# Attention loop: value and output products in halves of the array's rows, query and key products whole in one step

## The chip, the cores and the metric

The kernel runs on one core of a Trainium2 chip. The metric is the device time of one execution in microseconds (us), from start to end, as the median of several runs. A profile of one execution gives the start and length of every instruction on every engine: TensorE (PE for its products and transposes, PEld for its weight loads), VectorE (DVE), ScalarE (ACT), GpSimd (POOL) and SyncE (SP, which issues the transfers).

## The reference

Four layers follow each other, each on a layer-normalised input and added to it: A, B, A, B, with the same weights for both A and for both B. A is a linear attention with a learned feature map. B, which the change touches, is a causal attention over 4 segments of 512 tokens with 32 heads of 16, and a memory that carries what earlier segments held:

```python
for s in range(N):                                   # N = 4 segments of L = 512
    qs, ks, vs = q[:, :, s], k[:, :, s], v[:, :, s]  # x @ wq, x @ wk, x @ wv
    logits = jnp.einsum("bhqd,bhkd->bhqk", qs, ks) * scale + mask
    p = _softmax(logits, axis=-1)
    a_dot = jnp.einsum("bhqk,bhkd->bhqd", p, vs)
    pq = phi(qs)
    num = jnp.einsum("bhld,bhde->bhle", pq, M)
    den = jnp.einsum("bhld,bhd->bhl", pq, z)[..., None] + 1e-6
    o = g * num / den + (1.0 - g) * a_dot
    outs.append(o)
    pk = phi(ks)
    M = M + jnp.einsum("bhld,bhle->bhde", pk, vs)
    z = z + jnp.einsum("bhld->bhd", pk)
...
return o @ wo
```

## The kernel before

**Stages.** Layer A runs in two passes (`pass1`, `pass2`). Layer B is one hand-ordered loop, `LayerB.steps` (L1470), which also takes in the end of the layer A before it and, in the first of the two layers B, the beginning of the next layer A.

**The loop.** Each of the 4 segments has 4 chunks of 8 heads (128 features), and each chunk two halves (a half chunk, m, is 4 heads: 8 of them a segment, 32 a layer). A half chunk has R = 5 steps; step number k = 5m + j. In every step TensorE does first the query-key products of one piece (`attend`, into the two banks lg, from which ScalarE writes the exponentials P), then those of another piece nine steps ahead for the row maxima (`maxima`, into one bank each, mx and my, of which VectorE takes the maxima). These use 64 rows of the array (63 for the maxima) and come in pairs, one product in the upper and one in the lower half of the rows. Then come the effects due at this step, and the products that fill it.

**What fills the steps.** P times values (`weighted`, bank pv, in column strips of 32) stands in steps j = 0 and 2. The rest is set by the tables FIRST (segment 0), GAPS (segments 1 and 2), LAST and FINAL (segment 3 of the first and the second layer B). An entry "m.j" lists what step j of half chunk m does: q, k, v with a chunk or tile number are the query, key and value projections ("+" for those of the next segment), out the output product of the segment before, max the transpose of the row maxima, t the transpose of key features to tokens, m the update of the memory, a its reading, n and ln the next normalisation (whose last four calls transpose the normalised rows into columns, `columns`, L433), x the request of a residual tile. "/2" takes two quarters of a product: each product is 12 full-array matmuls of 512 columns (`mm3`, L482), four quarters of three, since each operand is kept as a high and a low part and three of the four combinations are summed. "~" puts the VectorE part of its end off into the next step.

**Orders.** All matmuls and transposes of TensorE are held in program order (`held`, L190); so are the instructions of VectorE, ScalarE, GpSimd and the SyncE queue (`Ordered`). The order in which a step issues its work is the order on each engine. In steps j = 2 the deferred VectorE parts (`late`) run before pv and the activations of key and query features (`later`) behind it.

**Banks.** The results of projections, output products, transposes, memory reads and updates share one pool of three PSUM banks, g (G = 3, L33). lg has two banks, mx, my and pv one each.

**Ends.** A projection (`proj`, L1043) ends with the load of the next weights, ScalarE's copy to the high part, VectorE's subtraction for the low part (ta), and, where the memory needs the features, two activations on ScalarE (tb) and two GpSimd instructions. A value product ends with a copy on ScalarE (`v_tile`, L531), an output product with an addition on VectorE and a store (`out`, L1420).

Of the kernel before, what the change touches and what calls it, by code (L numbers as in the profile page):

```python
# [7 lines left out]
F32 = mybir.dt.float32  # L8
# [69 lines left out]


FIRST = """  # L80
0.1 max k2/2 | 0.2 v3/2 | 0.3 k2/2~ | 0.4 v3/2
1.0 m0 | 1.1 max q3/2 | 1.3 q3/2~ | 1.4 t1 k3/1
2.1 max k3/3 | 2.2 m1 w | 2.3 ln~ | 2.4 ln~ ln~
3.1 ln~ max | 3.3 q0+/2 | 3.4 t2 q0+/2~ w
4.0 w | 4.1 max k0+/2 load | 4.2 m2 | 4.3 k0+/1 | 4.4 k0+/1
5.0 n | 5.1 max v0+/4 | 5.2 w | 5.3 q1+/2 n | 5.4 t3 q1+/2~
6.1 max v1+/4 | 6.2 m3 n | 6.3 k1+/2 | 6.4 a0+ k1+/2
7.0 n | 7.1 max q2+/4~ | 7.2 n | 7.3 v2+/2 n | 7.4 t0+ v2+/2
# [12 lines left out]
LAST = """  # L101
0.1 max k2/3~ | 0.2 n | 0.3 k2/1~ v3/2 n | 0.4 a1 v3/2 n
1.0 n | 1.1 max q3/3 n | 1.2 n | 1.3 q3/1~ k3/2 n | 1.4 k3/2~ n
2.1 max out/1 | 2.3 out/2 | 2.4 a2 x0 pre
3.1 max ln~ ln~ | 3.3 pre out/1 ln~ out/1 x1 | 3.4 out/1 ln~
4.1 max out/2~ v/2 | 4.3 pre out/3 x2 | 4.4 a3 out/1~ v/2 x3
5.1 max out/3 | 5.2 out/1 v/1 | 5.3 fin v/1 | 5.4 v/2 pre
6.1 max v/2 | 6.3 fin v/2 | 6.4 v/2
7.1 pt p/3 v/2 | 7.2 v/2 | 7.3 fin v/2 p/3 | 7.4 p/3
"""  # L110
FINAL = """
0.1 max k2/4~ | 0.3 v3/3 | 0.4 a1 v3/1~
1.1 max q3/2 | 1.3 q3/2~ | 1.4 k3/1
2.1 max k3/2 | 2.3 k3/1 out/1 pre | 2.4 a2 out/2 x0
3.0 x1 | 3.1 max | 3.3 pre out/2 | 3.4 out/2
4.1 max out/1~ | 4.3 pre out/2 x2 | 4.4 a3 out/2
5.1 x3 out/2 max | 5.3 fin out/2 | 5.4 pre
6.1 max | 6.3 fin
7.1 pt p/2 | 7.3 p/4 fin | 7.4 p/3
"""  # L120
BEFORE = {-25: "q0 load", -23: "v0", -21: "k0", -18: "n", -17: "v1 n", -16: "n", -15: "n n", -14: "q1 n", -13: "n", -12: "k1 n n", -10: "v2 n", -4: "max q2~", -1: "t0"}


@with_exitstack
def interleave_kernel(ctx, tc, x_in, a_wqkv, a_wphi, a_wo, b_wq, b_wk, b_wv, b_wo, b_beta,
# [15 lines left out]
    def nm(s):  # L141
        uid[0] += 1
        return f"{s}_{uid[0]}"
# [20 lines left out]
    def behind(i, j):  # L164

        tc.add_manual_dep(i.ins, j.ins.name,
                          mybir.DependencyInfo(mybir.DependencyClass.NoSync, mybir.DependencyReason.DATA),
                          reason="keeps order")

    class Ordered:  # L170

# [53 lines left out]
    gated = cp.tile([P, NC, 4], F32, name="gated")  # L225
    ones = cp.tile([32, P], F32, name="ones")
    stats = cp.tile([P, NT, 4], F32, name="stats")
    junk = cp.tile([P, 2, 384], mybir.dt.uint8, name="junk")

    def constants():  # L230
# [776 lines left out]
    class LayerB:  # L1007
# [21 lines left out]

        def values(self, s):  # L1030

            self.vv[s] = []
            yield from v_tile(self.hT[s], self.wv, self.vv[s], ("g", G), (0, 3, 1, 2), True)

        def queue_w(self):

            if self.wnext:
# [2 lines left out]
                dma(w, wqk[m][:, c])  # L1040
                self.w4.append(w)

        def proj(self, s, c, m):  # L1043

            d, hT, w = self.st.setdefault((s, c), {}), self.hT[s], self.w4.pop(0)
            pp = PS("g", G)
            yield from mm3(pp, lambda a, kc: w[:, a, kc, :], lambda b, kc: hT[b][:, kc, :])
            self.queue_w()
            hi, lo = d["part", m] = [T2("ta1", TA, F32R) for _ in range(2)]
            act.copy(hi, pp)  # L1050
            wait(lambda: dve.tensor_tensor(out=lo, in0=pp, in1=hi.bitcast(F32), op=SUB))
            if not (s == 0 if m == 0 else s == NSEG - 1):
                e = d["phi", m] = T2("tb2", TB2)
                r = T2("tb3", 2)

                def first():
                    act.activation(e, pp, AF.Exp)

                def second():
                    act.activation(r, pp, AF.Relu)  # L1060
                    pool.tensor_scalar(e, e, 1.0, None, op0=MIN)
                    pool.tensor_tensor(out=e, in0=e, in1=r, op=ADD)
                self.later += [first, (lambda: self.later.append(second)) if s < 2 else second]
            yield

        def at(self, k, f, *a):

# [351 lines left out]

        def out(self, s):  # L1420
            for t in range(4):
                po = PS("g", G)
                yield from self.product(po, s, t, range(NC))
# [5 lines left out]
                wait(end)  # L1429
                yield  # L1430

        def early(self):

# [18 lines left out]
                yield  # L1452

        def opening(self):
            self.w4 = []
            self.wo = []
            self.wnext = [(m, c) for _ in range(NSEG) for c in range(NC) for m in range(2)]
            for _ in range(2):
                self.queue_w()
                yield  # L1460
            self.wv = []
            yield from bring(self.wv, "bwv")
            self.norm0 = self.norm(0)
            next(self.norm0)
            fills = self.start()
            for n in (0, 0, 1, 0, 1, 0, 1, 1, 1, 1, 0, 1, 1, 1, 1, 1, 1, 1, 1):
                yield
                next(self.norm0 if n else fills, None)

        def steps(self, side, after, table_end):  # L1470
# [8 lines left out]
            outs, proj, part = {}, {}, {}  # L1479
            early = self.early()  # L1480

            def do(what, s, k):
                put_off[0] = self.late if what[-1] == "~" else None
# [8 lines left out]
                elif op == "fin":  # L1492
                    if k >= FINAT:
                        self.finish((k - FINAT) // R)
                elif op in ("q", "k", "v", "out", "p"):
                    if op == "p":
                        g = early
                    elif op == "out":
                        if s == 0:
                            return  # L1500
                        g = outs.setdefault(s, self.out(s - 1))
                    elif op == "v":
                        g = after if i is None else val[s]
                    else:
                        g = proj.setdefault((s, i, op), self.proj(s, i, "qk".index(op)))
# [56 lines left out]
            for k in range(BEGIN, R * N + 4):  # L1562
                m = k // R + 3
                if k % R == 0 and 0 <= m < N:
                    self.stack(m)
                if 0 <= k < R * N:
                    next(at)
                if -LEAD <= k < R * N - LEAD:
                    next(ma)
                put_off[0] = None  # L1570
                self.due(k)
                for s, c in memory["a"].get(k, ()):
                    if s > 0:
# [19 lines left out]
                what, s = table.get(k, ((), 0))  # L1593
# [73 lines left out]
```

## Time and profile before

| What | Value |
|---|---|
| median of 3 runs | 1403.85 us (1402.75 to 1408.85) |
| span of the profiled execution | 1401.3 us |
| instructions | 33234 |
| attention loop, first layer, four segments | 293.0 to 717.0 us |
| attention loop, second layer | 979.6 to 1388.7 us |
| granted TensorE clock | 1.00 throughout |

The profiled execution's span runs from its first to its last instruction; the 2.55 us between it and the median are what lies around it, and the spread of the runs. The costliest groups of the page are ScalarE's exponentials (324.5 us of busy time) and, on TensorE, the full-array products into g. Matmuls are pipelined: the busy time of a group counts an instruction from its start to the end of its results, so that the distance between two starts, not the length, says what an instruction costs TensorE.

### The profile page before, as it was taken

Reading aid. Unit: us, or ns where it says so; the run is one execution under the profiler, and the core shown is the slowest. Engines: PE = TensorE matmul, PEld = TensorE weight load, DVE = VectorE, ACT = ScalarE, POOL = GpSimd, SP = SyncE. Lnnn points to the kernel's source line nnn. Section 1 sums busy time; section 2 is a strip of 40 time slices with the busy share of each in tenths; the row PEclk is TensorE's granted clock in tenths of the full one; section 3 lists DMA queues with packets and bytes.
Section 4 is the critical chain, followed back from the end, with each engine's and each line's share of the span. In section 5 each row is a group of like instructions: output and inputs, shape, how many; then the busy total and the mean of one; then the engine's idle time right before and its main releaser. Section 6 shows DMA issues by size and latency. Waiting matters only on the chain.

```text
span 1401.3 us, 33234 instructions
## 1 busy us (share of the span) xinstructions
PE 1369.1 (98%) x12070; PEld 943.2 (67%) x12070; DVE 963.9 (69%) x3030; ACT 810.9 (58%) x1244; POOL 734.1 (52%) x1073
## 2 busy tenths in 40 slices
PE   9999999999999999999999999999999999999998
PEld 7787778766666666655568887886655666666554
DVE  5766888677667657667647768958776666666674
ACT  5555445447686677566544434553566866765654
POOL 1677755324656656554534346642356565754643
PEclk9999999999999999999999999999999999999999
DMA  5369285645756656567631104855465566565552
GB/s 199 118 216 330 99 280 175 187 122 162 201 131 190 169 137 183 158 171 196 197 134 39 62 31 125 275 162 155 137 172 171 148 178 180 143 172 142 155 158 69
DMA packets 135730, 225.27 MB, mean 161 GB/s; under 512 B 21328, under 2 KB 39888, under 8 KB 135568
## 3 DMA queue, kind: packets, MB, share of 16 engines
q1 hardware_dynamic: 134464, 222.91, 54.2%
q8 instruction: 97, 1.59, 0.5%
q14 instruction: 65, 0.53, 0.1%
q10 hardware_dynamic: 1104, 0.24, 0.1%
HBM read 116.39 MB, written 43.25 MB: 114 GB/s over the span
## 4 chain that ended last, share of the span: by engine, by line
PE 78%; DVE 8%; ACT 5%; POOL 4%; issue 2%; DMA 2%; SPq 0%; DVEq 0%; ACTq 0%; POOLq 0%
PE g L202 47%; PE pv L202 9%; PE lg L202 9%; PE mx L202 4%; PE g L206 3%; PE my L202 3%; ACT P L180 2%; PE lg L206 1%; POOL P L180 1%; POOL tb L180 1%; DVE es L180 1%; POOL tmp L180 1%; DVE junk L180 1%; DVE my L180 1%; DVE mx L180 1%
## 5 line engine op out<-in xcount | busy, mean ns | idle before, releaser
L180 ACT ACTIVATE P<-lg 128x1024 f32<-128x1024 f32 x316 | 324.5, 1027 | 167.5 <-PE lg L202 159.6
L180 POOL TENSOR_SCALAR_AFFINE_SELECT P<-P 128x256 f32<-128x256 f32 (+1 forms) x448 | 190.3, 439 | 388.9 <-ACT P L180 388.1
L180 DVE CUSTOM_DVE_ANT_0 junk<-mx,mask 128x128 uint8<-128x128 f32 (+2 forms) x384 | 146.6, 420 | 101.8 <-PE my L202 72.7
L202 PE MATMUL g<-hh,wqk 128*128 128x512 f32 x512 | 186.3, 411 | 0.7 <-ACT mt L180 0.7
L202 PE MATMUL lg<-e,e 64*128 64x512 f32 (+1 forms) x1010 | 166.0, 386 | 6.4 <-ACT P L180 6.0
L180 DVE CUSTOM_DVE_ANT_0 mx<-mx,mask 128x512 f32<-128x512 f32 x128 | 89.2, 697 | 120.1 <-PE my L202 95.4
L202 PE MATMUL g<-w,oh 128*128 128x512 f32 x508 | 169.2, 414 | 0.5 <-ACT hh L180 0.4
L202 PE MATMUL pv<-P,v 128*32 128x512 f32 (+3 forms) x2048 | 165.5, 439 | 0.6 <-ACT ot L180 0.5
L202 PE MATMUL my<-e,e 63*128 63x256 f32 (+3 forms) x519 | 147.2, 343 | 4.2 <-DVE mxs L180 3.0
L202 PEld LDWEIGHTS lg<-e,e 64*128 64x128 f32 x1010 | 79.9, 184 | 102.9 <-issue 44.9
L202 PE MATMUL mx<-e,e 63*128 63x256 f32 (+3 forms) x519 | 145.9, 334 | 1.9 <-DVE mxs L180 1.6
L180 DVE CUSTOM_DVE_ANT_0 junk<-my,mask 128x128 uint8<-128x128 f32 (+2 forms) x384 | 146.8, 420 | 0.0
L202 PE MATMUL g<-w,hh 128*128 128x512 f32 x448 | 143.9, 402 | 0.3 <-ACT hh L180 0.3
L202 PEld LDWEIGHTS pv<-P,v 128*32 128x32 f32 x2048 | 53.5, 109 | 102.9 <-issue 95.3
L202 PEld LDWEIGHTS g<-hh,wqk 128*128 128x128 f32 x512 | 96.2, 188 | 33.7 <-issue 13.4
L202 PEld LDWEIGHTS g<-w,oh 128*128 128x128 f32 x508 | 87.6, 189 | 30.8 <-issue 13.4
L202 PE MATMUL g<-w,ol 128*128 128x512 f32 x254 | 100.8, 397 | 2.3 <-DVE ol L180 2.2
L180 DVE DVE_READ_ACCUMULATOR2_ANT mxs<- 128x1 f32 x1024 | 100.4, 98 | 0.0
L202 PE MATMUL g<-hl,wqk 128*128 128x512 f32 x256 | 100.3, 392 | 0.0
L202 PEld LDWEIGHTS mx<-e,e 63*128 63x128 f32 (+1 forms) x519 | 90.8, 185 | 10.0 <-DVE mxs L180 5.0
L202 PEld LDWEIGHTS g<-w,hh 128*128 128x128 f32 x448 | 80.3, 188 | 22.6 <-issue 6.0
L202 PEld LDWEIGHTS my<-e,e 63*128 63x128 f32 (+1 forms) x519 | 84.2, 185 | 15.7 <-DVE mxs L180 8.3
(190 smaller groups left out, 2848.2 us busy)
## 6 DMA issues: line engine op xcount, KB each, us to landing
e<-ta SPq DMA_DIRECT2D x384, 128.0 KB
wqk<-wqk SPq DMA_DIRECT2D x64, 512.0 KB
x<-x SPq DMA_DIRECT2D x48, 256.0 KB
xr<-x SPq DMA_DIRECT2D x32, 256.0 KB
x<-xr SPq DMA_DIRECT2D x28, 256.0 KB
tmp<-U SPq DMA_DIRECT2D x56, 128.0 KB
KN<-inv SPq DMA_DIRECT2D x28, 256.0 KB
pq<-tb SPq DMA_DIRECT2D x24, 256.0 KB
```

The source lines that it names most:

```text
L180: i = f(*a, **k)
L202: return held(nc.tensor.matmul(*a, **k))
L206: return held(nc.tensor.transpose(*a))
```

## The change

Value products and output products of the loop are done in halves (`split`). The contraction over 128 rows is cut into two of 64, the 512 result columns into two of 256 with a bank of g each. One matmul takes the upper 64 rows into the first bank while another takes the lower 64 rows into the second; after four units the rows are turned, so that each bank gets the other half of the contraction. A job has 8 units of three pairs, 48 matmuls where there were 12. Its end adds or copies each half by itself; a value tile's halves are copied by ScalarE and by VectorE.

Between the last pair of one turn and the first of the next, a one-element VectorE copy (`passed`, `marked`) keeps matmuls from other rows out of a bank that is still being written.

The units (u in the tables) stand in steps 3 and 4, and, in some, at the end of step 2 or 0 of a neighbouring half chunk; there they are issued ahead of pv. Query and key products stay whole and mostly take one step, j = 1, in which the transposes (max, t, some ln) stand too. The order of the jobs is that of JOBS; "/" marks an output job that leaves the first turn of the last chunk to its end.

```diff
-0.1 max k2/3 | 0.2 n | 0.3 k2/1~ v3/2 | 0.4 a1 v3/2
-1.0 m0 n n | 1.1 max q3/3 | 1.2 n q3/1~ | 1.3 k3/2 | 1.4 t1 k3/2~
-2.1 max out/3 | 2.2 m1 | 2.3 ln ln | 2.4 a2 ln x0
-3.1 max ln out/1~ | 3.3 q0+/3 x1 | 3.4 t2 q0+/1~ k0+/2
-4.1 max k0+/2~ out/1 load | 4.2 m2 | 4.3 out/3~ x2 | 4.4 a3 q1+/4~
-5.0 n | 5.1 max out/3 | 5.3 out/1 v0+/2 n x3 | 5.4 t3 v0+/2 k1+/1
-6.1 k1+/3~ max | 6.2 m3 | 6.3 out/3 | 6.4 a0+ out/1 v1+/2
-7.0 n n | 7.1 max v1+/2 q2+/1 begin | 7.2 n | 7.3 q2+/3~ n N | 7.4 t0+ v2+/4 N
+0.1 max k2/4~ | 0.2 n | 0.3 u/4 | 0.4 a1 u/4
+1.0 m0 n n | 1.1 max t1 q3/2 | 1.2 n | 1.3 q3/2~ | 1.4 k3/2
+2.0 m1 | 2.1 max k3/2~ ln ln | 2.3 u/3 | 2.4 a2 u/3 x0
+3.0 ln ln | 3.1 u/1 max t2 q0+/4~ x1 | 3.2 u/1 | 3.3 u/4 | 3.4 u/4
+4.0 m2 | 4.1 max k0+/4~ load | 4.3 u/4 x2 | 4.4 a3 u/4
+5.0 n | 5.1 max t3 q1+/4~ | 5.3 u/4 n x3 | 5.4 u/4
+6.0 m3 | 6.1 max k1+/4~ | 6.2 u/4 | 6.3 u/4 | 6.4 a0+ u/4
+7.0 n n u/4 | 7.1 max t0+ q2+/4~ begin | 7.2 n | 7.3 u/4 n N | 7.4 u/4 N
...
-4.1 max out/2~ v/2 | 4.3 pre out/3 x2 | 4.4 a3 out/1~ v/2 x3
+4.1 x3 ln~ ln~ max v/2 | 4.2 u/4 | 4.3 pre u/4 | 4.4 a3 u/4
...
+JOBS = ("v v+ v+ v+", "v out/ out out out v+ v+ v+", "v out/ out out out")
...
+    def passed():
+
+        if last_half[0] is not None:
+            tick[0] = dve.tensor_copy(beat, bd[0:1, 0:1])
+            sync_on(tick[0], last_half[0])
+            last_half[0] = None
+
+    def marked(i):
+
+        assert last_half[0] is None
+        sync_on(i, tick[0])
...
+        def split(self, job, late=False):
+
+
+            lhs, rhs, _, end = job
+            po = [PS("g", G)[:, 0:256] for _ in range(2)]
+            order = [(p, kc) for p in range(2) for kc in range(NC)]
+            if late:
+                order.append(order.pop(NC - 1))
+            for step, (turned, kc) in enumerate(order):
+                for n, (a, b) in enumerate(((0, 0), (0, 1), (1, 0))):
+                    for j in range(2):
+                        h = (j + turned) % 2
+                        rows = slice(64 * h, 64 * h + 64)
+                        i = mm(po[j], lhsT=lhs(a, kc)[rows], rhs=rhs(b, kc)[rows, 256 * j : 256 * j + 256],
+                               start=(step == 0 and n == 0), stop=(step == 7 and n == 2), tile_position=(64 * h, 0))
+                        if step and n == 0 and turned != order[step - 1][0]:
+                            marked(i)
+                        if j and n == 2 and step < 7 and turned != order[step + 1][0]:
+                            last_half[0] = i
+                if step == 7:
+                    end(*po)
+                yield
...
-                def end(po=po, t=t):
+                def summed(p0, p1, t=t):
                     x = self.xq.pop(0)
-                    dve.tensor_tensor(out=x, in0=po, in1=x, op=ADD)
+                    for j, p in enumerate((p0, p1)):
+                        half = x[:, 256 * j : 256 * j + 256]
+                        dve.tensor_tensor(out=half, in0=p, in1=half, op=ADD)
                     sync.dma_start(out=self.xdst[4 * s + t], in_=x)
...
+                passed()
                 if 0 <= k < R * N:
                     next(at)
                 if -LEAD <= k < R * N - LEAD:
                     next(ma)
+                what, s = table.get(k, ((), 0))
+                if k in weights:
+                    for w in what:
+                        if w.startswith("u"):
+                            do(w, s, k)
+                    what = [w for w in what if not w.startswith("u")]
```

The tables of the other segments change in the same way: units in steps 3 and 4 and whole query and key products in step 1.

More of the change, by code (lines that the diff above doesn't have):

```diff
@@ L80 @@
 FIRST = """
[L81 to L88, printed above, removed]
+0.1 max k2/4~ | 0.3 u/4 | 0.4 u/4
+1.0 m0 | 1.1 max t1 q3/2 | 1.3 q3/2~ | 1.4 k3/1
@@ L110 @@
 """
 FINAL = """
[L112 to L117, printed above, removed]
+0.1 max k2/4~ | 0.3 u/4 | 0.4 a1 u/4
+1.1 max q3/2 | 1.3 q3/2~ | 1.4 k3/2
+2.1 max k3/2~ | 2.3 u/3 pre | 2.4 a2 u/3 x0
+3.1 u/1 max | 3.2 u/1 x1 | 3.3 pre u/4 x2 | 3.4 u/4
+4.1 max x3 | 4.2 u/4 | 4.3 pre u/4 | 4.4 a3 u/4
@@ L118 @@
+5.0 u/4 | 5.1 max | 5.3 fin | 5.4 pre
 6.1 max | 6.3 fin
@@ L168, in behind, with sync_on @@
                           reason="keeps order")
+    last_half, tick = [None], [None]
+    def sync_on(i, j):
+        tc.add_manual_dep(i.ins, j.ins.name,
+                          mybir.DependencyInfo(mybir.DependencyClass.Sync, mybir.DependencyReason.DATA),
+                          reason="other rows of the array write the same bank")
+    def passed():
[6 more added lines that the diff above has]
+        sync_on(i, tick[0])
     class Ordered:
@@ L227, in interleave_kernel @@
     stats = cp.tile([P, NT, 4], F32, name="stats")
+    beat = cp.tile([1, 1], F32, name="beat")
     junk = cp.tile([P, 2, 384], mybir.dt.uint8, name="junk")
@@ L1041, in queue_w, with whole @@
                 self.w4.append(w)
+        def whole(self, job):
+            lhs, rhs, end, _ = job
+            po = PS("g", G)
+            yield from mm3(po, lhs, rhs)
+            end(po)
+            yield
[18 more added lines that the diff above has]
+                    end(*po)
+                yield
@@ L1043, in proj @@
         def proj(self, s, c, m):
             d, hT, w = self.st.setdefault((s, c), {}), self.hT[s], self.w4.pop(0)
[L1046 to L1063, printed above, removed]
@@ L1064, in proj, with parts, end, first @@
-            yield
+            wanted = not (s == 0 if m == 0 else s == NSEG - 1)
+            def parts():
+                d["part", m] = [T2("ta1", TA, F32R) for _ in range(2)]
+                if wanted:
+                    d["phi", m] = T2("tb2", TB2)
+                return d["part", m]
+            def end(pp):
+                self.queue_w()
+                hi, lo = parts()
+                act.copy(hi, pp)
+                wait(lambda: dve.tensor_tensor(out=lo, in0=pp, in1=hi.bitcast(F32), op=SUB))
+                if wanted:
+                    e, r = d["phi", m], T2("tb3", 2)
+                    def first():
+                        act.activation(e, pp, AF.Exp)
+                    def second():
+                        act.activation(r, pp, AF.Relu)
+                        pool.tensor_scalar(e, e, 1.0, None, op0=MIN)
+                        pool.tensor_tensor(out=e, in0=e, in1=r, op=ADD)
+                    self.later += [first, (lambda: self.later.append(second)) if s < 2 else second]
@@ L1066, in at @@
+            return lambda a, kc: w[:, a, kc, :], lambda b, kc: hT[b][:, kc, :], end, None
         def at(self, k, f, *a):
@@ L1478, in steps, with job, units @@
             val = [self.values(s) for s in range(NSEG)]
-            outs, proj, part = {}, {}, {}
+            outs = [None] + [self.out(s) for s in range(NSEG - 1)]
+            whole, part = {}, {}
             early = self.early()
+            def job(name, s):
+                s += name[-1] == "+"
+                name = name.rstrip("+")
+                if name == "out":
+                    return next(outs[s])
+                if name[0] == "v":
+                    return next(val[s])
+                return self.proj(s, int(name[1]), "qk".index(name[0]))
+            def units():
+                for s in range(NSEG):
+                    for name in JOBS[0 if s == 0 else 1 if s < NSEG - 1 else 2].split():
+                        yield from self.split(job(name.rstrip("/"), s), name[-1] == "/")
+            units = units()
             def do(what, s, k):
@@ L1494, in do @@
                         self.finish((k - FINAT) // R)
-                elif op in ("q", "k", "v", "out", "p"):
+                elif op == "u":
+                    for _ in range(int(quarters)):
+                        next(units)
+                elif op in ("q", "k", "v", "p"):
                     if op == "p":
                         g = early
[L1498 to L1503, printed above, removed]
-                    else:
-                        g = proj.setdefault((s, i, op), self.proj(s, i, "qk".index(op)))
+                    elif i is None:
+                        g = after
+                    else:
+                        if (s, what) not in whole:
+                            whole[s, what] = self.whole(job(what, s))
+                        g = whole[s, what]
                     n = int(quarters) if quarters else (3 if op == "p" else 4) - part.pop(op, 0) % 4
```

45 lines of the change are left out of this document (31 added, 14 removed).

## The prediction

> I write m.j for step j (0 to 4) of half chunk m (0 to 7) of a segment, as the tables of the kernel do.
>
> **What bounds the kernel now.** I read the page first: its busy shares, then the chain that ended last.
>
> ```profile
> span 1401.3 us, 33234 instructions
> PE 1369.1 (98%) x12070; PEld 943.2 (67%) x12070; DVE 963.9 (69%) x3030; ACT 810.9 (58%) x1244; POOL 734.1 (52%) x1073
> PE 78%; DVE 8%; ACT 5%; POOL 4%; issue 2%; DMA 2%; SPq 0%; DVEq 0%; ACTq 0%; POOLq 0%
> ```
>
> TensorE holds the chain. A busy share of 98% does not say that it does useful work all that time, so next I cut the attention loop into its segments (first layer: segments 0, 1, 2, then segment 3 of the last layer; columns: stretch, length, busy time of each engine).
>
> ```profile
> 293.00:393.00 100.00, 98.43 (x824) 61.26 (x826) 70.32 (x285) 66.18 (x98) 48.90 (x84) 1.00 0.56 159
> 393.00:501.30 108.30, 107.66 (x888) 66.92 (x887) 70.44 (x281) 74.54 (x110) 63.62 (x103) 1.00 0.61 167
> 501.30:610.10 108.80, 107.85 (x886) 66.98 (x884) 71.28 (x282) 71.81 (x104) 62.68 (x102) 1.00 0.60 165
> 1296.70:1388.70 92.00, 88.06 (x660) 49.40 (x659) 59.06 (x220) 54.58 (x75) 49.62 (x77) 1.00 0.50 132
> ```
>
> The middle segments take 108 to 109 us each, and there are four of them in the two layers. VectorE and ScalarE are at two thirds. So TensorE is the bound, but the others have only a third to spare. The timeline of TensorE for one half chunk (start, length, what; pv is step 2, the second lg is step 3, the third is step 4) shows what its time is spent on:
>
> ```profile
> 519.87 0.56 PE L202 MATMUL lg<-e,e 64*128 64x256 f32 x4
> 520.27 0.40 PE L202 MATMUL mx<-e,e 63*128 63x512 f32 x1
> ...
> 520.60 1.28 PE L202 MATMUL pv<-P,v 128*32 128x384 f32 x16
> 521.81 0.50 PE L202 MATMUL g<-hh,wqk 128*128 128x512 f32 x1
> ...
> 522.70 0.57 PE L202 MATMUL lg<-e,e 64*128 64x256 f32 x4
> 523.10 0.28 PE L202 MATMUL mx<-e,e 63*128 63x256 f32 x1
> ...
> 523.22 0.33 PE L202 MATMUL mx<-e,e 63*128 63x384 f32 x1
> ...
> 523.49 0.50 PE L202 MATMUL g<-hh,wqk 128*128 128x512 f32 x1
> 523.83 0.39 PE L202 MATMUL g<-hl,wqk 128*128 128x512 f32 x1
> 524.06 0.62 PE L202 MATMUL g<-hh,wqk 128*128 128x512 f32 x2
> 524.52 0.40 PE L202 MATMUL g<-hl,wqk 128*128 128x512 f32 x1
> 524.76 0.40 PE L202 MATMUL g<-hh,wqk 128*128 128x512 f32 x1
> 525.08 0.50 PE L202 MATMUL lg<-e,e 64*128 64x256 f32 x4
> 525.42 0.28 PE L202 MATMUL mx<-e,e 63*128 63x256 f32 x1
> ...
> 525.54 0.28 PE L202 MATMUL mx<-e,e 63*128 63x256 f32 x1
> ...
> 525.75 0.66 PE L206 MATMUL g<-ident,tb 128*128 128x128 f32 x4
> ```
>
> Read the starts, not the lengths. A full-array product of 512 columns follows the last one by 0.23 us (523.83, 524.06, and 524.52 to 524.76). A pair of 64-row products of 256 columns, one in each half of the rows, follows by 0.12 (525.42 to 525.54). A change between the two shapes costs extra, twice each way. Into full rows: 523.22 to 523.49 is 0.27, where the 384 columns need some 0.17 (0.12 x 384/256, rounded), so 0.09 is lost; then 523.49 to 523.83 is 0.34 instead of 0.23, 0.11 lost. Back: 524.76 to 525.08 is 0.32 instead of 0.23, 0.09 lost; then the two pairs from 525.08 take 0.34 instead of 0.24, 0.10 lost. **One change of shape costs 0.2 us, a visit 0.39.** Nothing else separates these instructions: there is no wait in this stretch.
>
> [...]
>
> **The change, part by part.** *Mode changes.* Before, every step of a middle segment has two: steps 0 and 2 for pv, the others for products or transposes; with one more where a product stands behind pv (1.2) that is 81 in 40 steps. After, steps 3 and 4 hold only halves, in the shape of lg and mx, except 1.3 and 1.4: 14 steps lose both, and 3.0 gets one more (normalised columns transposed behind pv): 53. Counted in the same way from the tables: first segment 78 to 57; last segment of layer one 82 to 64, of layer two 77 to 60. In all 21+28+28+18 and 21+28+28+17 = 189 fewer, by 0.2: **-37.8 us**.
>
> *Halves.* A whole product is 12 x 0.2325 (four follow each other from 523.83 to 524.76) = 2.79. A split one is 24 pairs by 0.12 = 2.88. 4+8+8+5 = 25 jobs a layer, 50 in all, by 0.09: **+4.5 us**. The longest chain of pairs in the trace has four, the new ones twelve or more, so the cadence is bounded by 0.12 (a pair behind a pair) and 0.22 (a pair behind a change); I take 0.12, since mx behind lg holds it, and keep the other end as a rival.
>
> *The third bank.* The pool g has three PSUM banks. A split job holds two, from its first unit to its end. Most jobs fill exactly steps 3 and 4, where at most one other tile of g is asked for. One does not: in a middle segment the output job runs from 2.3 to 3.2, and 3.0 and 3.1 now hold two columns, the maxima's transpose, the tokens' transpose and a whole query product, five tiles in turn through one bank. Each must be emptied before the next starts. Their chain before, with three banks (second half of a step 1; and a token copy from ScalarE's timeline):
>
> ```profile
> 543.72 0.60 PE L206 MATMUL g<-ident,x 128*128 128x128 f32 x4
> 543.97 0.27 ACT L180 ACTIVATE mt<-g 16x128 fp32r<-16x128 f32 x1 [0.34 <-PE g L206]
> 544.36 0.59 ACT L180 CAST hh<-g 128x512 fp32r<-128x512 f32 x1
> 544.98 0.69 DVE L180 TENSOR_TENSOR hl<-g,hh 128x512 fp32r<-128x512 f32 x1
> ```
>
> ```profile
> 526.89 0.58 ACT L180 COPY tb<-g 128x512 f32<-128x512 f32 x1
> ```
>
> A column is emptied 1.95 us after its transposes began (543.72 to 544.98, and 0.69), while they hold TensorE for 0.44 (four by 0.11): the second column waits 1.5. The maxima's transpose finds the bank busy for 1.95 again, less 0.44, lg 0.43, mx 0.30 and a unit of 0.36: 0.4. The tokens wait for mt, 0.35 + 0.27: 0.6. The query product waits for the tokens' copy, 0.64 + 0.58 less 0.44: 0.8. Sum 3.3, four times, and some 2 us in the last segment of layer one, where layer A's value product holds the third bank beside a job: **+15 us**. From below it is nothing if these engines have emptied the bank by then, which the rows exclude for the second column (6 us for the four); from above each wait is longer by an exponential (1.03) ahead of it on ScalarE.
>
> [...]
>
> *Steps 2 to 4.* Whole products make step 1 long (4 us and more), so the work of VectorE and ScalarE meets shorter steps 2 to 4. In those they had this to do in the same half chunk:
>
> ```profile
> 520.70 0.70 DVE L180 CUSTOM_DVE_ANT_0 mx<-mx,mask 128x512 f32<-128x512 f32 x1 [1.67 <-PE my L202]
> ...
> 521.97 0.95 DVE L180 RECIPROCAL dn<-dn 128x128 f32<-128x128 f32 x1
> 523.59 0.29 DVE L180 CUSTOM_DVE_ANT_0 junk<-mx,mask 128x128 uint8<-128x128 f32 x1 [0.68 <-PE my L202]
> ...
> 524.98 0.08 DVE L180 DVE_READ_ACCUMULATOR2_ANT mxs<- 128x1 f32 x1
> 525.40 0.69 DVE L180 TENSOR_TENSOR ta<-g,ta 128x512 fp32r<-128x512 f32 x1 [0.34 <-ACT tb L180]
> ```
>
> ```profile
> 520.47 1.02 ACT L180 ACTIVATE P<-lg 128x1024 f32<-128x1024 f32 x1 [0.84 <-PE lg L202]
> 521.95 0.69 ACT L180 ACTIVATE U<-pv,share 128x512 f32<-128x512 f32 x1 [0.45 <-PE pv L202]
> ...
> 523.37 1.03 ACT L180 ACTIVATE P<-lg 128x1024 f32<-128x1024 f32 x1
> 524.29 1.08 ACT L180 ACTIVATE tb<-g 128x512 f32<-128x512 f32 x2
> ```
>
> Count from lg of step 2 (519.87 = 0). TensorE after: pv ends at 1.94; lg of step 3, 0.40; mx, 0.30; four units, 1.43: step 4 begins at 4.07 and wants the maxima's banks at 4.3. VectorE: the row maxima start at 0.83 and end at 2.1; the reciprocal to 3.0; the subtraction ta, which now always falls here because its product ends in step 1, to 3.7; the maxima of step 3 take 523.59 to 525.06, 1.47: banks free at 5.1. TensorE waits 0.8. ScalarE: U ends at 2.77, the two activations tb (1.08) at 3.85, the exponential of step 3 at 4.9: lg of step 4 waits 0.8 too, at the same time. One cause is enough. Before, step 3 and 4 took 522.70 to 527.74 and hid it. Going through the half chunks of a middle segment, five or six have the wait of 0.8, and 1 and 2 about 0.6 each for normalised rows: 6 us with what 3.3 to 3.4 loses. But the counted TensorE work of a middle segment before is 105.2 (64 quarter products of three by 0.2325, 44.6; lg and mx 8 x 2.55; pv 16 x 1.1, from 520.60 to 521.81 less a half change; small products and transposes 6.4; changes 81 by 0.2) against 108.6 measured: 3.4 of waits are already there. So +2.6 a segment, four times: **+10 us**. In the first segment whole products move from light half chunks to one with no slack in steps 2 to 4; a step cannot be under the maxima's cycle (mx at 520.27 to 522.1, 1.85), so I count back 3 of its 4 us, twice: **+6 us**.
>
> *Small things.* The tick: a one-element VectorE instruction, 56 of them, must come behind the last half and ahead of the first turned one. It stands in VectorE's queue ahead of the next maxima, which come later on TensorE anyway, and TensorE waits for it only behind lg and mx of the next step (0.5): nothing, or at most 0.1 each, 5 us, where VectorE is late. The sum of two halves: one subtraction of 512 is 0.69, two halves between that and twice that, at a step's end: inside the terms above. SyncE: each product still issues its one weight load at its end, up to three steps earlier, and the residual rows are asked for at most a step earlier: no cost, the tile is wanted a half chunk later. GpSimd keeps its work; its order moves by a step and its share of 52% covers that.
>
> **The sum.** -37.8 + 4.5 + 15 + 10 + 6 = -2.3 on the profiled execution. Its span is 1401.3; the median shown, 1403.85, is 2.55 more, which I carry along unchanged. **1401.5 us.** What a run of this kernel can tell from no change is about 0.5%, 7 us.
>
> **The rivals.** *The waits hide* (0.27). VectorE and ScalarE have a third of their time free; if their queues run ahead and the bank is emptied sooner, the full -33.3 lands, 1370.5; with the part of the bank's wait that a row demands (6) it is 1376.5, with half of the rest too 1389. For it: TensorE's timeline shows no wait. Against it: steps 2 to 4 by the rows.
>
> *One bank and a late VectorE* (0.19, the other side): the new waits do not replace the 3.4 us that a middle segment has but add to them, since those sit elsewhere (4 x 3.4 = 14): 1415. It decides from the point at which a middle segment loses 11.7 us to waits (3.4 now, 6 + 3.3 in my forecast): from there it is slower by 0.5%. For it: five tiles through one bank at 3.0 and 3.1, all in TensorE's own order.
>
> *Loads in turn* (0.04).
>
> ```profile
> L202 PEld LDWEIGHTS lg<-e,e 64*128 64x128 f32 x1010 | 79.9, 184 | 102.9 <-issue 44.9
> L202 PEld LDWEIGHTS g<-hh,wqk 128*128 128x128 f32 x512 | 96.2, 188 | 33.7 <-issue 13.4
> ```
>
> A half load takes as long as a whole one, 184 against 188 ns, and there are four times as many. If a long chain could not overlap them, a pair would cost the 0.22 of one behind a change: 24 x 0.10 = 2.4 more a job, 50 jobs: 1520. The busy time of the 64-row loads, 79.9/1010 = 0.08 each, says that they overlap.
>
> [...]
>
> **How the numbers follow.** Forecast 0.50, from 1390 to 1412: within 0.5% (1396.8 to 1410.9) in 0.34, below in 0.12, above in 0.04. With the rivals: faster 0.39, same 0.34, slower 0.27. The range leaves out a tenth on either side: 1376 to 1416.
>
> **What would show it.** Some 1800 more matmuls, most of the new ones 64*128 by 256 columns with starts 0.12 apart; 0.22 would be the loads. Middle segments of 108 to 109 us; 104 would mean that the waits hide, 112 the slower rival. In 3.0 and 3.1 TensorE idle ahead of transposes behind hl, hh, mt and tb, 3 us in each middle segment; if it is not there, the bank's term is wrong. In step 4, lg and mx waiting for P and mxs by some 0.8. I am wrong if a change of shape turns out cheaper than 0.2 where halves stand beside lg, or if VectorE's queue has more slack in steps 2 to 4 than one half chunk shows.

## The result, and the profile after

The changed kernel takes **1453.07 us** (median of 4 runs, 1450.39 to 1458.43) against 1403.68 (1402.75 to 1408.85) of the kernel before on the same chip: a ratio of 1.0348, 95% interval 1.0320 to 1.0376. It is slower by 49 us. The prediction was 1401.5 with a range that ended at 1416.

The page of the changed kernel, first its span and busy shares, then the chain that ended last:

```profile
span 1452.3 us, 36952 instructions
...
PE 1365.0 (94%) x13870; PEld 999.6 (69%) x13870; DVE 979.4 (67%) x3136; ACT 807.8 (56%) x1244; POOL 733.2 (50%) x1073
...
PE 68%; DVE 11%; ACT 7%; DMA 5%; issue 3%; POOL 3%; SPq 2%; DVEq 0%; ACTq 0%; POOLq 0%
```

There are 1800 more matmuls, yet TensorE is busy for 4 us less (1369.1 before), in a span that is 51 us longer. Its share of the last chain went from 78% to 68%. So TensorE did not get slower: it waits. The segments of the first layer B show where (stretch, length, busy time of PE, PEld, DVE, ACT, POOL, granted clock, DMA share, GB/s):

```profile
293.00:393.50 100.50, 96.12 (x964) 64.94 (x962) 72.25 (x292) 65.02 (x98) 47.76 (x84) 1.00 0.57 158
393.50:511.10 117.60, 106.57 (x1178) 74.69 (x1176) 72.92 (x299) 74.10 (x111) 64.86 (x103) 1.00 0.57 155
511.10:630.90 119.80, 107.53 (x1174) 76.62 (x1172) 73.37 (x298) 71.90 (x105) 63.01 (x102) 0.97 0.55 150
630.90:747.00 116.10, 106.02 (x905) 69.27 (x907) 67.36 (x258) 64.48 (x92) 50.20 (x84) 0.94 0.54 152
```

The first segment is nearly as it was. The middle ones take 118 to 120 instead of 108 to 109 (117 to 118 in the second layer B), and the last one 116 instead of 104, counted to the last product P times values. In the middle ones PE's busy time is 11 to 12 short of the length; before it was under 1 short. The clock is no longer 1.00 everywhere, to which I come back.

What TensorE's matmuls wait for (us in total, times, longest), whole program, of the changed kernel:

```profile
PE lg L223 <- ACT P L201: 32.8, 34, 1.8
PE pv L223 <- ACT ot L201: 8.7, 6, 1.7
PE g L227 <- DVE hl L201: 7.1, 9, 1.4
PE my L223 <- DVE mxs L201: 4.0, 18, 0.3
PE g L223 <- ACT tb L201: 3.3, 5, 0.7
```

and the first of these rows in the kernel before:

```profile
PE lg L202 <- ACT P L180: 6.0, 16, 0.9
```

To count this by stage I took each step from the start of one TensorE instruction to the next, and summed what exceeds the largest step of the waitless stretches (0.35 us after a full product, 0.36 after a 64-row one, 0.21 after a transpose, 0.47 after pv; the longer steps of a memory read are left aside). In the four middle segments of the two layers, 434.6 us before and 472.4 after, that is 1.8 before and 48.5 after:

| place, middle segments | before | after |
|---|---|---|
| lg of step 4 behind the exponential of step 3 | 0.0 | 22.5 (24 times) |
| five tiles through one bank in 3.0 and 3.1 | 0 | 11.8 |
| pv behind the memory read and GpSimd | 0.3 | 9.6 |
| the rest | 1.5 | 4.6 |

So 46.7 us of waits were added. The length without waits fell by 8.9, from 432.8 to 423.9: the gain is there, but the added waits are five times as large.

**The first wait** is a chain over two engines. The timeline of the changed kernel around one step 4:

```profile
473.77 0.56 PE L223 MATMUL lg<-e,e 64*128 64x256 f32 x4
473.91 0.69 ACT L201 ACTIVATE U<-pv,share 128x512 f32<-128x512 f32 x1 [0.45 <-PE pv L223]
...
473.93 0.95 DVE L201 RECIPROCAL dn<-dn 128x128 f32<-128x128 f32 x1
...
474.47 0.45 PE L223 MATMUL g<-w,oh 64*128 64x256 f32 x4
...
474.71 0.33 PE L223 MATMUL g<-w,ol 64*128 64x256 f32 x2
...
474.80 0.63 DVE L201 TENSOR_TENSOR ta<-g,ta 128x512 fp32r<-128x512 f32 x1
...
475.46 1.09 ACT L201 ACTIVATE tb<-g 128x512 f32<-128x512 f32 x2 [0.86 <-DVE ta L201]
...
475.55 0.45 PE L223 MATMUL g<-w,oh 64*128 64x256 f32 x4
...
475.78 0.33 PE L223 MATMUL g<-w,ol 64*128 64x256 f32 x2
...
476.43 1.03 ACT L201 ACTIVATE P<-lg 128x1024 f32<-128x1024 f32 x1
...
477.51 0.50 PE L223 MATMUL lg<-e,e 64*128 64x256 f32 x4 [1.40 <-ACT P L201]
```

Read it backwards. lg of step 4 (477.51) waits for the exponential of step 3, whose lg was done at 474.33. The exponential starts only at 476.43, behind the two activations tb. These start at 475.46, for ScalarE stood idle for 0.86 us until VectorE's ta was done; and ta stands behind the reciprocal. The prediction counted VectorE and ScalarE side by side; here they work in turn.

**The second wait**, TensorE's timeline around 3.0 and 3.1 of the changed kernel:

```profile
433.02 0.66 PE L227 MATMUL g<-ident,x 128*128 128x128 f32 x4
435.07 0.66 PE L227 MATMUL g<-ident,x 128*128 128x128 f32 x4 [1.40 <-DVE hl L201]
...
437.13 0.28 PE L227 MATMUL g<-ident,mxs 128*16 128x128 f32 x1 [0.33 <-DVE hl L201]
437.81 0.66 PE L227 MATMUL g<-ident,tb 128*128 128x128 f32 x4 [0.40 <-ACT mt L201]
439.15 0.50 PE L223 MATMUL g<-hh,wqk 128*128 128x512 f32 x1 [0.68 <-ACT tb L201]
```

These are the four waits that the prediction gave for the third bank, in their order, for hl, hl, mt and tb. Together they are 2.8 us in brackets; 3.3 were predicted.

**The third wait**, the changed kernel at a memory read:

```profile
463.40 1.29 POOL L201 TENSOR_TENSOR tmp<-tmp,ot 128x512 f32<-128x512 f32 x1
...
464.73 0.62 ACT L201 CAST oh<-tmp 128x512 fp32r<-128x512 f32 x1 [1.83 <-POOL tmp L201]
...
465.25 0.68 ACT L201 ACTIVATE ot<-pv,bd 68x512 f32<-68x512 f32 x1
...
466.08 1.28 PE L223 MATMUL pv<-P,v 128*32 128x512 f32 x16 [1.33 <-ACT ot L201]
```

ScalarE's cast of the joined output waits 1.83 us for GpSimd and holds up the activation ot behind it, which reads the bank pv that the next pv writes. The prediction did not have this one.

### The profile page after: what moved, and what is told of

Its sections match the earlier page's. It is cut to its first block, busy times and chain, and to the rows that moved or that the text cites. A ratio compares the mean times of both kernels' runs of the same rounds, so it can differ in the third digit from the quotient of the medians.

```text
span 1452.3 us, 36952 instructions
## 1 busy us (share of the span) xinstructions
PE 1365.0 (94%) x13870; PEld 999.6 (69%) x13870; DVE 979.4 (67%) x3136; ACT 807.8 (56%) x1244; POOL 733.2 (50%) x1073
## 4 chain that ended last, share of the span: by engine, by line
PE 68%; DVE 11%; ACT 7%; DMA 5%; issue 3%; POOL 3%; SPq 2%; DVEq 0%; ACTq 0%; POOLq 0%
PE g L223 42%; PE pv L223 7%; PE lg L223 7%; PE mx L223 4%; PE g L227 3%; ACT P L201 3%; PE my L223 2%; SPq L201 2%; DMA e<-ta 2%; DVE my L201 2%; ACT tb L201 2%; PE lg L227 1%; DVE ta L201 1%; DMA xr<-x 1%; POOL P L201 1%
## 5 line engine op out<-in xcount | busy, mean ns | idle before, releaser
L223 PE MATMUL g<-w,oh 64*128 64x256 f32 (+1 forms) x1084 | 189.4, 335 | 6.5 <-ACT mmq L201 3.1
L223 PE MATMUL g<-hh,wqk 128*128 128x512 f32 x512 | 181.5, 411 | 3.4 <-ACT tb L201 2.7
L223 PE MATMUL g<-w,hh 64*128 64x256 f32 (+1 forms) x1072 | 159.7, 314 | 1.0 <-ACT mt L201 0.8
L223 PEld LDWEIGHTS lg<-e,e 64*128 64x128 f32 x1010 | 83.2, 186 | 111.0 <-ACT P L201 71.2
L223 PEld LDWEIGHTS g<-w,oh 64*128 64x128 f32 (+1 forms) x1084 | 128.0, 195 | 29.7 <-issue 11.4
L223 PE MATMUL g<-w,ol 64*128 64x256 f32 (+1 forms) x542 | 128.6, 322 | 3.0 <-DVE ol L201 2.2
L223 PEld LDWEIGHTS g<-w,hh 64*128 64x128 f32 (+1 forms) x1072 | 115.4, 187 | 15.8 <-issue 4.2
L223 PE MATMUL g<-w,hl 64*128 64x256 f32 (+1 forms) x536 | 111.7, 304 | 0.0
L201 ACT CAST ta<-g 128x512 fp32r<-128x512 f32 x64 | 37.5, 586 | 114.6 <-PE g L223 106.3
L201 POOL TENSOR_SCALAR tb<-tb 128x512 f32<-128x512 f32 x48 | 71.4, 1487 | 58.7 <-ACT tb L201 58.7
```

Source lines behind the costliest of these rows:

```text
L201: i = f(*a, **k)
L223: return held(nc.tensor.matmul(*a, **k))
```

## The experiments

All kernels below compute the whole result. Ratios are to the kernel before, which had medians of 1402.86 to 1404.33 us in these comparisons. The first four change one thing in the changed kernel.

**Halves or order?** The order of the changed kernel, with its jobs on full rows: the split jobs run as 12 full products in the same eight units, into one bank, without a tick. The end still adds or copies two halves.

```diff
 def split(self, job, late=False):
     lhs, rhs, _, end = job
+    if True:
+        pw = PS("g", G)
+        seq = [(kc, n, a, b) for kc in range(NC) for n, (a, b) in enumerate(((0, 0), (0, 1), (1, 0)))]
+        for unit in range(8):
+            for _ in range(2 - unit % 2):
+                kc, n, a, b = seq.pop(0)
+                mm(pw, lhsT=lhs(a, kc), rhs=rhs(b, kc), ...)
+            if unit == 7:
+                end(pw[:, 0:256], pw[:, 256:512])
+            yield
+        return
```

> The changed tables stay, but the units of value and output products are done as full-array matmuls of 512 columns again (12 a job over its 8 units, one bank of g, no tick). Theory 'waits' (the halves save what was counted, the new order loses it in waits): the mode changes come back (+37.6), the pairs' extra goes (-4.5), the third bank is free (-15 with the half-clock windows behind it), and step 4's waits for the exponential shrink by the 0.4 us that steps 3 and 4 get longer (about -10): 1453 + 8 = 1461, between 1450 and 1475. Rival 'halves' (the halves themselves cost the time, by loads, tick or evacuation): back to before, 1404 to 1415.

1438.44 us, ratio 1.0261 [1.0235, 1.0288]. This is neither theory's number. A middle segment has 80 changes of shape here, as many as before (counted in the trace), so nothing is saved there, and the time is 35 us above the kernel before: this is the price of the order, with whole products packed into step 1. The middle segments take 463.1 with 30.9 of waits, of which 21 are lg behind the exponential. The halves add another 14.6 to the time.

**Features later.** Both activations tb of a product put into step 3.

```diff
-self.later += [first, (lambda: self.later.append(second)) if s < 2 else second]
+self.later.append(lambda: self.later.extend([first, second]))
```

> The two feature activations of a query or key product (tb) are both done in step 3, behind its exponential, instead of step 2 (or 2 and 3). Theory 'waits': TensorE's idle time before lg behind P (22 us in the middle segments of both layers, and the half-clock windows it helps to cause) mostly goes, 1453 - 22 + some 2 = 1430, between 1422 and 1440. Rival 'halves': no change, 1453 within 5. Rival 'VectorE's queue in steps 2 to 4 is the wait' (maxima behind reciprocal and ta): the wait moves from P to mxs and at most 5 us are won.

1442.74 us, 1.0283 [1.0262, 1.0303]. In the middle segments the 22.5 us of lg behind the exponential are gone, and yet the time fell by only 10: there pv now waits 14.8 for ot (8.9 in the changed kernel), and my, one bank of the maxima, 6.5. A wait that is taken away lets the next one show.

**The output job on full rows.** Only the first output job of a segment, which lies across 3.0 and 3.1, goes into one bank, so that two are left for the five tiles.

```diff
 lhs, rhs, _, end = job
+if late:
+    pw = PS("g", G)
+    ...
```

> Only the first output job of each segment (2.3 to 3.2) is done with full-array matmuls in one bank, so that 3.0 and 3.1 have two banks of g. Theory 'waits': the chain of waits between columns, maxima's transpose, tokens and query product goes (11.7 us in four segments, predicted as 13), with it most of the half-clock windows that begin there (three of eight, some 5 us), while 4 mode changes a segment come back (+5): 1453 - 12 = 1441, between 1435 and 1447. Rival (the bank is emptied in time, the waits there are the other engines'): 1453 + 5.

1437.64 us, 1.0235 [1.0203, 1.0266]: as expected, 15.4 less. The waits at 3.0 and 3.1 fall from 11.8 to 0.5 (the middle segments to 454.9, their waits to 34.3). The prediction had +15 for the third bank; this run also has no half clock left in the middle segments, where the changed kernel spent 10.2 us at it (told under the hardware below).

**The cast later.** GpSimd's join is followed by ScalarE's cast one step later in the middle segments.

```diff
-JOIN = (..., ((9.5, 9.5, 11.5, 12, 13.5),) * 4, ...)
+JOIN = (..., ((9.5, 9.5, 11.5, 13, 13.5),) * 4, ...)
```

> In the middle segments the cast of a joined output (oh, which waits for GpSimd) is due one step later, at step 0 instead of 4, so that it no longer stands ahead of the memory read's two activations in ScalarE's queue. Theory 'waits': TensorE's wait of pv behind the read (9.6 us in the middle segments) goes mostly: 1445, between 1442 and 1449. Rival (GpSimd itself holds the read's tiles): 1453 within 2.

1448.45 us, 1.0325 [1.0306, 1.0343]: within the expectation, though the interval overlaps that of the changed kernel. In the middle segments pv waits 5.3 for ot instead of 8.9, so the cast was part of it and not all.

**The three together.**

> The three single edits together: both feature activations in step 3, the first output job of a segment on full rows, the cast one step later. Single gains were 10, 15 and 5. Theory 'waits' with independent places: 1453 - 30 = 1423, between 1418 and 1430. Rival 'GpSimd is next' (in the run with the activations later, 4 us of pv waits came up behind the selections that GpSimd makes after the two feature instructions): the sum falls short, 1430 to 1438.

1427.59 us, 1.0167 [1.0132, 1.0202]. Alone they gave 10.3, 15.4 and 4.6, together 25.5. The middle segments take 442.7 (434.6 before), 19.3 of it waits.

**GpSimd's share of the features moved as well**, to the next step 1, out of the way of the masks and joins.

```diff
 def second():
     act.activation(r, pp, AF.Relu)
-    pool.tensor_scalar(e, e, 1.0, None, op0=MIN)
-    pool.tensor_tensor(out=e, in0=e, in1=r, op=ADD)
+    self.later.append(lambda: self.later.append(lambda: self.later.append(joined)))
+def joined():
+    pool.tensor_scalar(e, e, 1.0, None, op0=MIN)
+    pool.tensor_tensor(out=e, in0=e, in1=r, op=ADD)
```

> As the three edits together, and GpSimd's two feature instructions (2.8 us) moved to the next step 1, the long one. Theory 'waits': with lg behind P (22.5), pv behind P and ot (9.6 to 14) and the one-bank chain (12) gone, and half-clock windows with them (9), it comes to 1453 - 52 = 1401, between 1395 and 1412. Rival 'GpSimd is not what pv waits for': as the three edits, about 1423.

1425.47 us, 1.0146 [1.0112, 1.0181]: 2 less than with the three edits, which the runs do not tell from nothing; 22 less were expected. GpSimd was what pv waited for, as the wait for ot falls from 9.4 to 2.5; but mx now waits 5.6 for VectorE instead of 1.9, so that VectorE is the one that is late.

**The same with all jobs on full rows** (the first experiment's edit instead of the third's).

> The same later activations, GpSimd order and cast, but all value and output jobs on full rows as in e1. It tells what the halves are worth once the waits are gone. Theory 'a change of shape costs 0.2': some 160 changes more than e8 (32) less the pairs' extra (4): e8 + 28, about 1430; where waits still hide part, e8 + 10 to 20. Rival 'the halves save nothing': as e8, within 5.

1432.38 us, 1.0190 [1.0150, 1.0230]. The halves are now worth 7 us by the medians, but the two intervals overlap, so the runs alone do not show a gain. The traces, one execution each, have the middle segments at 448.0 on full rows and at 440.5 in halves. That is less than expected: the kernel on full rows waits less in them (10.7 against 17.5 in the four).

**The last segment of layer one.** It had grown to 114 to 121 us. Layer A's value product starts a half chunk later, when the read's banks are free.

```diff
-4.1 x3 ln~ ln~ max v/2 | 4.2 u/4 | ...
-5.0 u/4 | 5.1 max v/4 | ...
+4.1 x3 ln~ ln~ max | 4.2 u/4 | ...
+5.0 u/4 | 5.1 max v/6 | ...
```

> As e8, and in the last segment of layer one the value product of the next layer A does not begin in 4.1 but in 5.1, so that its bank is free beside the jobs of 4.2 to 4.4. Theory 'third bank': the 3 us wait of the halves behind the memory read in 4.4 and a half-clock window of 6.8 us there go: e8 - 6, between -3 and -9. Rival (the read waits for GpSimd, not for the bank): e8 within 2.

1420.06 us, 1.0105 [1.0073, 1.0138]: 5.4 less by the medians, with intervals that overlap, and in the traces that segment went from 114.3 to 108.4.

VectorE now idled ahead of the additions to the residual rows xr until these rows had landed. The total (us, times) and one of these places in the timeline, both of this last kernel:

```profile
  DMA xr<-x: 10.7, 6
```

```profile
585.70 0.76 DVE L201 TENSOR_TENSOR xr<-g,xr 128x256 f32<-128x256 f32 x2 [1.65 <-DMA xr<-x]
...
586.37 0.69 DVE L201 CUSTOM_DVE_ANT_0 mx<-mx,mask 128x512 f32<-128x512 f32 x1
...
587.17 0.38 PE L223 MATMUL mx<-e,e 63*128 63x256 f32 x1 [0.64 <-DVE mxs L201]
```

The rows are late, the row maxima are behind them in VectorE's queue, and TensorE's mx waits for these. The row is asked for in 5.3 and its output job now ends in 5.4; before, that job ended in 6.4.

**Rows earlier**, in the kernel of the last run.

```diff
-... 1.4 k3/2 | ... 2.4 a2 u/3 x0 | 3.1 ... x1 | ... 4.3 u/4 x2 | ... 5.3 u/4 n x3
+... 1.4 k3/2 x0 | ... 2.4 a2 u/3 x1 | ... 3.3 u/4 x2 | ... 4.3 u/4 x3 | ... 5.3 u/4 n
```

> The kernel of the run with the later last segment (1420.1), with the residual rows asked for one to five steps earlier in the middle segments (x0 at 1.4, x1 at 2.4, x2 at 3.3, x3 at 4.3). In that kernel VectorE sat idle for 10.7 us in front of additions to xr whose rows had not landed; four of the six cases are the row that is asked for in 5.3 and wanted in 5.4. Theory 'rows too late': those 10.7 go, and the part of them that stood ahead of maxima reaches TensorE, 4 to 9 us: 1411 to 1416, with less waiting for the maxima's banks in step 1 of half chunk 6. Rival 'off the path': VectorE merely idles elsewhere, 1418 to 1422.

1407.02 us, 1.0029 [1.0011, 1.0046]: 13 less, more than either theory allowed. The middle segments are at 430.3, 4.3 under the kernel before, with 10.5 of waits (16.3 in the run above) and no time at half clock, of which the run above had 6.8 us there (the last section tells of it).

**The subtraction ta at once**, in all tables of the changed kernel: is it VectorE that holds up tb?

```diff
-... 3.1 u/1 max t2 q0+/4~ x1 | ... 4.1 max k0+/4~ load | ... 5.1 max t3 q1+/4~ | ...
+... 3.1 u/1 max t2 q0+/4 x1 | ... 4.1 max k0+/4 load | ... 5.1 max t3 q1+/4 | ...
```

> The changed kernel (1453.1), with one thing different: VectorE's subtraction ta of a product that ends in step 1 is no longer put off to step 2 but issued at once. Theory 'ScalarE waits for VectorE': in the changed kernel the two feature activations tb stand behind that subtraction, which stands behind the reciprocal, and the exponential of step 3 stands behind tb; without this the 22.5 us for which lg of step 4 waits behind P in the middle segments fall to some 10, and the time is 1437 to 1445. Rival 'ScalarE alone': U, two tb and an exponential fill ScalarE whatever VectorE does, the waits stay, 1450 to 1456. Third case: the subtraction, now ahead of the row maxima of step 1, delays them by 0.65 us, and the time rises above 1456.

1453.17 us, 1.0357 [1.0337, 1.0376]: no change. This is the number of the rival, but not for the rival's reason. TensorE's waits, and ScalarE's for ta, of this kernel:

```profile
PE lg L223 <- ACT P L201: 13.5, 23, 1.1
PE my L223 <- DVE mxs L201: 9.3, 46, 0.3
```

```profile
ACT tb L201 <- DVE ta L201: 6.1, 8, 0.8
```

ScalarE's wait for ta fell to 6.1 us (19.8 in the changed kernel) and lg's wait in the middle segments from 22.5 to 4.8: the chain was read rightly. But the middle segments fell by only 5.7, to 466.7. The subtraction now stands ahead of the row maxima, and what it gave came back there (my, 4.0 to 9.3) and in the first segments, 205.4 instead of 200.6. The waits are those of the first theory and of the third case at once.

**Both of these edits**, in the kernel with the later last segment.

> The kernel of the run with the later last segment (1420.1) with both edits of this call: residual rows earlier, and ta at once. The feature activations are in step 3 here, so ta at once is worth less than in the changed kernel: 1406 to 1416 by both theories, 1418 to 1424 by both rivals. Whether it comes down to the kernel before (1403.7) is what is asked.

1414.15 us, 1.0079 [1.0064, 1.0094]. 7 more than with the rows alone: the middle segments stay (431.3), the first ones go from 201.1 to 207.0.

**The last segments as before.** The kernel with earlier rows, but with the tables of both last segments, their quarter jobs and whole output products put back.

> The kernel of the run with earlier residual rows (1407.0), whose four middle segments are the changed ones, with the tables of the last segments of both layers put back to those of the kernel before (quarter jobs, whole output and value products). In that kernel the last segments take 109.2 and 90.8 us where the kernel before has 104.3 and 89.5. Theory 'the last segment has no slack for halves': they come back to 104 to 105 and 89 to 90, 5 to 7 less in all, 1400 to 1402.5: level with the kernel before (about 1404 in these runs) or 2 to 4 us below it. Rival 'it is what the middle segments hand over' (the feature instructions put later, the memory reads): the last segments stay at 107 or more, 1405 to 1409.

**1400.70 us, 0.9976 [0.9963, 0.9989]**: the only kernel here that is faster than the one before, by a quarter of a per cent, with an interval that lies below 1. Its middle and last segments in layer one (columns as above):

```profile
394.00:501.20 107.20, 105.68 (x1142) 73.95 (x1140) 73.17 (x297) 73.26 (x111) 64.14 (x105) 1.00 0.61 166
501.20:608.70 107.50, 104.88 (x1138) 73.33 (x1136) 72.94 (x296) 70.80 (x104) 62.70 (x99) 1.00 0.62 171
608.70:715.80 107.10, 102.08 (x718) 59.92 (x716) 66.83 (x247) 64.70 (x91) 52.37 (x85) 0.98 0.57 164
```

The time is as the first theory had it, but the last segment came back only to 107.1 (104.3 before), which was the rival's sign. Of these 2.8 us up to 1.7 are half clock, of which 3.4 us lie in that segment. Whether the remainder is handed over by the middle segments or comes from the later feature activations, which hold here too, no run tells apart.

**Rows earlier alone**, in the changed kernel itself.

> The changed kernel itself (1453.1) with nothing but the residual rows asked for earlier. Theory 'masked': VectorE idles only 3.4 us in front of additions to xr in the changed kernel, since TensorE is late by its other waits, so it gains 0 to 4 us: 1449 to 1454. Rival 'a loss of its own': the 13 us that the same edit took from the improved kernel are there too, 1438 to 1445.

1452.05 us, 1.0341 [1.0319, 1.0363]: nothing that can be measured, where the same edit took 13 us from the improved kernel. The larger losses hid this one.

The main runs side by side, from their traces (four middle segments, their waits as counted above, what is left, both last segments):

| kernel | time | middle | waits | left | last |
|---|---|---|---|---|---|
| before | 1403.7 | 434.6 | 1.8 | 432.8 | 104.3 + 89.5 |
| changed | 1453.1 | 472.4 | 48.5 | 423.9 | 116.0 + 89.8 |
| order on full rows | 1438.4 | 463.1 | 30.9 | 432.2 | 107.5 + 89.4 |
| three edits | 1427.6 | 442.7 | 19.3 | 423.4 | 121.5 + 90.3 |
| and last segment | 1420.1 | 440.5 | 16.3 | 424.2 | 108.4 + 92.8 |
| and rows earlier | 1407.0 | 430.3 | 10.5 | 419.8 | 109.2 + 90.8 |
| last as before | 1400.7 | 429.9 | 9.7 | 420.2 | 107.1 + 90.5 |

## Why the prediction was wrong

*Mode changes (from one of the two shapes to the other), -37.8.* The count held: 189 fewer in the loops of the trace (630 to 441), as predicted. The size was a little too large. In the kernel of 1400.7 us, with no half clock in its middle segments, 96 fewer changes and 28 split jobs should have saved 96 x 0.2 - 28 x 0.09 = 16.7 there; the column "left" fell by 12.6. If the jobs cost what was said, a change cost 0.16 net, not 0.2. The changed kernel's middle segments got only 8.9 of the 19.5 that were forecast for them (112 x 0.2 less 32 x 0.09). Of the 10.6 that are missing, 4.5 are this price (112 x 0.04) and up to 5.1 the half clock, of which 10.2 us lie there.

*Halves, +4.5.* Right. In the timeline of the first wait two pairs (474.47, x4) are followed by the next after 0.24, and again at 475.55 and 475.78 (0.23) far on in the same chain: 0.12 a pair. The rival with loads in turn (1520) is out.

*The third bank, +15.* Right: 13.2 were predicted for the middle segments and 11.8 measured, in the order of waits that the prediction gave. The run that gave the five tiles a second bank gained 15.4.

*Steps 2 to 4, +10: this step failed.* In place of 10 there were 35 us in the middle segments (46.7 less the bank's 11.8), for three reasons.
- The 3.4 us per middle segment that were "already there" did not exist. They were the residue of a count (108.6 less 105.2), and the trace before has 0.45 of waits a segment (1.8 / 4). That alone is 12 us.
- The wait of 0.8 was counted on two engines side by side. They are chained (tb waits for ta), and lg of step 4 waited for 0.94 on average (22.5 in 24 cases, six a segment where five or six were counted). That this size came out near is partly luck, as the path to it was another; the wait of mx and my for VectorE, which was to be as long, was small (1.7 for both in the middle segments).
- The memory reads' pv, 9.6, was not looked for. Of GpSimd the prediction said only that "its share of 52% covers that", but its instructions stand in that very chain.

*The tick.* Right: the products into g of the changed kernel waited 0.6 us for it, in two cases.

*First segments, +6.* With its fewer mode changes and eight jobs (-8.4, +0.7) the prediction came to -1.7 there; measured is 199.5 to 200.6, +1.1.

*Last segments.* Predicted about -4 (35 fewer changes, ten jobs, +2 for the bank). Layer one's took 11.7 more, layer two's 0.3. Moving the value product and putting the old tables back won most of it back, so it belongs for the most part to the halves and the layer A work there. Of these 11.7, up to 6.8 are half clock, of which 13.7 us lie in that segment.

*Residual rows, "no cost".* Wrong in its reason: the output job ends a half chunk earlier while the row is asked for at the same time, so that for the last row of a segment the slack went from six steps to one. It cost nothing in this kernel, since all else was later, and 13 us when it was not.

*The sum.* Middle segments +37.7 instead of +4, first +1.1 instead of -1.7, last +12.0 instead of -4: 50.8 of the 51.0 by which the span grew. The slower rival, *One bank and a late VectorE*, was the right one, and it named its point: 11.7 us of waits a middle segment. There were 12.1. Its price of 1415 was far too low, because it, too, took 3.4 of these as present before, and had neither the last segment nor the half clock.

## What to carry to other kernels

When work is moved into a step, follow the chain link by link over all engines, in the half chunk with the most side work, and ask also in which order two engines read the same bank (ScalarE's tb stood idle for 19.8 us behind VectorE's ta here). That each engine has a third of its time free says nothing about it. A residue between counted work and a measured length is uncounted work until a row shows a wait. A wait that is removed uncovers the next one in the queue, and an edit without any effect in the changed kernel (the earlier rows) gained 13 us once the others were made.

## What the runs showed of the hardware

The granted clock fell to half in the changed kernel, in stretches of 3.4 us (one of 6.8), 27.3 us in all, none of it in the kernel before until its very end. The stretch before such a one, the one itself, the next, and a second place (columns as above) in the changed kernel:

```profile
557.70:561.10 3.40, 1.99 (x13) 1.24 (x10) 1.89 (x10) 1.52 (x3) 0.41 (x1) 1.00 0.01 2
561.10:564.50 3.40, 3.40 (x10) 2.52 (x8) 0.00 (x0) 0.00 (x0) 0.00 (x0) 0.50 0.00 0
564.50:567.90 3.40, 3.40 (x41) 2.15 (x41) 2.29 (x7) 2.21 (x3) 0.76 (x2) 1.00 0.51 129
697.70:701.10 3.40, 1.46 (x11) 0.72 (x9) 2.04 (x10) 1.22 (x2) 2.03 (x3) 0.99 0.41 151
701.10:707.90 6.80, 5.68 (x48) 5.58 (x50) 1.55 (x5) 2.59 (x4) 0.96 (x2) 0.50 0.04 12
```

TensorE's timeline inside the first of them:

```profile
561.82 1.05 PE L223 MATMUL g<-hh,wqk 128*128 128x512 f32 x2
562.67 0.63 PE L223 MATMUL g<-hl,wqk 128*128 128x512 f32 x1
563.10 1.05 PE L223 MATMUL g<-hh,wqk 128*128 128x512 f32 x2
563.96 0.63 PE L223 MATMUL g<-hl,wqk 128*128 128x512 f32 x1
```

Full products now start 0.43 apart (562.67 to 563.10) instead of 0.23. The place is the one where five tiles pass through one bank: the waits there leave TensorE busy for 1.99 of 3.40 us, and the query product behind them pays again. The stretches of the changed kernel begin at 561.1, 571.3, 673.7, 690.8, 701.1 (the one of 6.8), 1158.4 and 1417.9 us, and between two starts lie whole multiples of 3.413 us (3, 30, 5, 3, 134 and 76 of them). I cut the traces of the two kernels along this grid (in the kernel before laid from its one stretch, at the end), from 300 us on and without the last 5 us, and took the windows that ran at full clock themselves. In the changed kernel, of 4 with TensorE busy for less than half, 3 were followed by half clock; of 40 between 0.5 and 0.8, 4; of 283 above, none. The kernel before has none under half, and none of its 6 between 0.5 and 0.8 was followed by it. The longest single gap sorts them no better: in the changed kernel 3 of the 5 windows with one over 1.5 us were followed by half clock, and so were 4 that had none over 0.7. So a wait cost more than its length where such a stretch followed it: at most 13.7 us here (half of 27.3). What in the window ahead brings it on is not shown: the 7 were busy for 0.37 to 0.79 of their time, 37 others of less than 0.8 kept the full clock, and no run changed the busy share alone.
